# Laying a fallback program ahead of the main code, and moving set-up off VectorE, in a fused attention and gated-MLP kernel

## The chip, the cores and the metric

The kernel runs on one core of one Trainium2 chip. The metric is the device time of one execution in microseconds (us). A figure with "median" is the median of several executions on the chip; every figure taken from a trace belongs to one profiled execution and counts from the start of its span. In the lines of the profile PE is TensorE, PEld its weight loads, ACT ScalarE, DVE VectorE, POOL GpSimd and SP SyncE, which in this kernel only issues transfers; PSUM is the memory of the tiles that the profile calls `ps`, which the matmuls write here (`PE MATMUL ps<-...`). TensorE's clock is a share of full speed, 1.0 or 0.5 in these traces, as the trace records it. A fetch is a packet that the trace lists on a queue of the kind "instruction", 8 or 16 KB each within the span; the 16 KB ones that stand beside jumps are put down to TensorE.

## The reference, cut to what matters

```python
x  = A_x                                  # (1, 2048, 512) bf16
xn = layernorm(x)
return x + attention(xn, wqkv, wo) + gated_mlp(xn, w1, w3, w2)
# attention: 32 heads of 16, softmax over 2048 keys
# gated_mlp: (silu(xn @ w1) * (xn @ w3)) @ w2, inner size 1792
```

The softmax needs 32 x 2048 x 2048 exponentials. The kernel computes most of them on ScalarE (790 instructions of 128x1024) and the rest (234) on VectorE with an integer approximation. That approximation is only right for scores in a range, so the kernel holds a second, slower and exact program, the fallback, and a flag that tells at the end which result stands. With these inputs the fallback is never run.

## The kernel before: the parts that matter

A planner in Python simulates the five engines with a table of durations and decides, before the kernel is built, in which order each engine's instructions stand. Its state is a clock and, for each engine, the time when it is free. It is greedy: what is ready first is placed first.

```python
class _Sched(_Prog):
    def __init__(self):
        ...
        self.free = {e: 0.0 for e in _ENGS}
    ...
    def _time(self, op, deps, dur, tail, mode=None, rows=None):
        ready = self._ready(op, deps)
        if op.eng != "pe":
            start = max(self.free[op.eng], ready)
            ...
```

The set-up, at the very start, is put on VectorE: a matrix of ones for TensorE's warm-up, the clear of a PSUM bank, three small mask operations, and a probe of what VectorE makes of 70000 in an integer conversion.

```python
P.op("dve", lambda e: e.memset(ones_t[:, :], 1.0), writes=[("ones_t",)], dur=0.1)
P.op("dve", lambda e: e.memset(bank(7), 0.0), writes=[("ps", 7)], dur=0.6)
# ... three mask operations, then the probe:
P.op("dve", lambda e: e.memset(satv[:, :], 70000.0), writes=[("satv",)], dur=0.1)
P.op("dve", lambda e: e.tensor_scalar(satn[:, :], satv[:, :], YB, G_LO, ALU.add, ALU.max), ...)
P.op("dve", lambda e: e.tensor_scalar(accb[:, 3:4], satn[:, :], 32767.0, None, ALU.is_equal), ...)
# ...
keep_warm(WARM, 0.107)      # warm-up matmuls for TensorE's clock
```

SyncE issues all loads and stores from one queue, in the planned order, and waits in that queue (in the profile before for up to 2.33 us at a time). Two kinds of issue matter below: the weights of the MLP in pairs, and the broadcast of the softmax's reciprocals, which has to wait until a small transfer, Rrow, has landed.

```python
def load_w13(idx):          # a pair of weight loads
    P.dma(lambda e: e.dma_start(w13[:, sl, 0:DC, :], w1_v[...]), writes=[("w13", sl, 0)], kb=128)
    P.dma(lambda e: e.dma_start(w13[:, sl, DC:2 * DC, :], w3_v[...]), writes=[("w13", sl, 1)], kb=128)

def e4():                   # a group of four broadcasts
    for j in range(4):
        q = P.dma(lambda e, j=j: e.dma_start(R[...], Rrow[j:j + 1, :]...broadcast_to([1, 16, 512])),
                  reads=[("Rrow",)], writes=[("R", j, h)], kb=32)
```

At the end every engine loads the flag and jumps over its part of the fallback, which lies between its main code and its end:

```python
def run(name, e):
    PF.emit_engine(name, e, sems[0][0], sems[0][1])          # main code
    e.wait_ge(sems[0][0]["dve"], flag_op.token[1])
    reg = e.alloc_register("slow_" + name)
    e.reg_load(reg, flag[0:1, 0:1])
    with e.If(e.snap(reg) > 0):
        ...                                                  # fallback
    PF.emit_end(name, e, sems[0][1])                         # SyncE waits for the outputs here
```

## Time and profile before

| | value |
|---|---|
| median of three runs, before the prediction | 787.33 us (785.9 to 787.77) |
| medians of the kernel before in the later jobs | 787.11, 787.61, 787.33, 787.62, 787.25 us |
| profiled execution | 785.95 us, span 784.14 us |
| TensorE's first real work, a transpose | 6.82 us |
| first exponential on ScalarE | 11.77 us |
| last VectorE operation to the end of the span | 5.18 us |

The lines of this profile that carry the argument stand in the prediction.

### The profile page before, as it was taken

The page shows a single profiled execution, that of the slowest core. Times are in us where ns is not written, and L with a number is a line of the kernel's source. Part 1 is how long each engine was busy: PE and PEld are TensorE (multiplying, and loading weights), DVE is VectorE, ACT ScalarE, POOL GpSimd, SP SyncE. Part 2 cuts the span into 40 slices and gives each one's busy share as a digit, 9 for nine tenths or more (in the row PEclk, how much of TensorE's full clock was granted, in tenths as well). Part 3 has the DMA queues.
Part 4 walks back from the last instruction along what each step waited for, and adds up shares of the span by engine and source line. Part 5 has one row for each costly group of instructions (what it writes and reads, how often), then busy time and mean ns, then how long its engine had stood idle before and what let it go on. Part 6 is the DMA issues. An engine that isn't in the chain of part 4 may idle for free.

```text
span 784.1 us, 21514 instructions
## 1 busy us (share of the span) xinstructions
PE 735.2 (94%) x9361; PEld 233.0 (30%) x9361; DVE 761.3 (97%) x872; ACT 764.2 (97%) x865; POOL 93.7 (12%) x120
## 2 busy tenths in 40 slices
PE   8999999999999999998899999998898999999996
PEld 6422222222222222222222322222222232222234
DVE  8899999999999999999999999999999999999995
ACT  6999999999999999999999999999999999999994
POOL 3200031102011020301102020110200202110000
PEclk9999999999999999999999999999999999999998
DMA  7023123213342213333403223332332212332202
GB/s 216 3 22 117 7 29 36 33 28 48 47 55 16 40 20 49 48 36 50 61 17 42 36 30 49 48 41 45 36 49 29 42 24 36 50 44 20 15 19 45
DMA packets 83440, 32.93 MB, mean 42 GB/s; under 512 B 72072, under 2 KB 79496, under 8 KB 83336
## 3 DMA queue, kind: packets, MB, share of 16 engines
q1 hardware_dynamic: 83336, 31.46, 28.0%
q8 instruction: 75, 1.23, 0.7%
q14 instruction: 29, 0.24, 0.1%
HBM read 22.81 MB, written 2.10 MB: 32 GB/s over the span
## 4 chain that ended last, share of the span: by engine, by line
ACT 82%; PE 10%; DVE 6%; issue 1%; DMA 0%; POOL 0%; DVEq 0%; ACTq 0%
ACT f_PT L1879 78%; PE ps L1338 3%; ACT f_th L1564 3%; PE ps L1809 3%; PE ps L2083 2%; DVE f_xd L1956 2%; DVE f_xd L2005 1%; DVE f_xd L1998 1%; DVE f_xd L2014 1%; DVE f_t L1568 0%; DVE f_hT L1578 0%; DMA f_xd<-in_A_x_dram 0%; DVE f_xd L2020 0%; PE ps L1350 0%; DVE f_stats L1262 0%
## 5 line engine op out<-in xcount | busy, mean ns | idle before, releaser
L1879 ACT ACTIVATE f_PT<-ps 128x1024 bf16<-128x1024 f32 x790 | 737.9, 1107 | 2.1 <-PE ps L1809 2.0
L1809 PE MATMUL ps<-f_QT,f_KT 32*128 32x512 bf16 (+1 forms) x2112 | 292.8, 378 | 29.6 <-ACT f_PT L1879 23.2
L1956 DVE TENSOR_SCALAR f_xd<-ps 128x1024 int16<-128x1024 f32 x234 | 284.6, 1216 | 7.1 <-PE ps L1809 7.0
L2083 PE MATMUL ps<-f_PT,f_Vaug 128*17 128x512 bf16 (+2 forms) x1628 | 208.8, 377 | 6.0 <-DVE f_xd L2005 2.2
L2083 PE MATMUL ps<-f_xd,f_Vaug 128*17 128x512 bf16 (+2 forms) x1452 | 196.2, 376 | 2.1 <-DVE f_U L2103 1.2
L1809 PEld LDWEIGHTS ps<-f_QT,f_KT 32*128 32x128 bf16 x2112 | 75.4, 91 | 305.5 <-ACT f_PT L1879 237.5
L1338 PE MATMUL ps<-f_xnT,f_w 128*32 128x512 bf16 x1792 | 137.1, 383 | 2.9 <-DVE f_t L1568 1.5
L2005 DVE TENSOR_TENSOR f_xd<-f_xd 128x3072 bf16<-128x3072 bf16 (+1 forms) x79 | 137.3, 1738 | 0.0
L1480 POOL TENSOR_SCALAR f_QT<-f_QT,f_msk 128x256 bf16<-128x256 bf16 x60 | 57.9, 965 | 292.6 <-DVE f_xd L2020 88.7
L1998 DVE TENSOR_SCALAR f_xd<-f_xd 128x3072 int16<-128x3072 int16 (+1 forms) x79 | 74.8, 947 | 1.1
L2083 PEld LDWEIGHTS ps<-f_PT,f_Vaug 128*17 128x17 bf16 (+1 forms) x1628 | 54.2, 92 | 69.9 <-issue 37.8
L2014 DVE TENSOR_SCALAR f_xd<-f_xd 128x3072 int16<-128x3072 int16 (+1 forms) x79 | 74.4, 942 | 0.0
L2020 DVE TENSOR_SCALAR f_xd<-f_xd 128x3072 int16<-128x3072 int16 (+1 forms) x79 | 74.2, 939 | 0.0
L1338 PE MATMUL ps<-f_w,f_hT 128*32 128x512 bf16 x896 | 71.5, 383 | 0.0
L2144 POOL TENSOR_TENSOR f_onorm<-f_U,f_R 128x256 bf16<-128x256 f32 x30 | 25.3, 850 | 344.7 <-DMA f_R<-f_Rrow 262.7
L2083 PEld LDWEIGHTS ps<-f_xd,f_Vaug 128*32 128x32 bf16 (+1 forms) x1452 | 50.5, 92 | 52.3 <-issue 32.8
L1338 PEld LDWEIGHTS ps<-f_xnT,f_w 128*32 128x32 bf16 x1792 | 39.2, 94 | 59.3 <-issue 44.2
L1578 DVE SCALAR_TENSOR_TENSOR f_hT<-f_t,ps 128x512 bf16<-128x512 bf16 x56 | 37.9, 676 | 0.2
L1568 DVE SCALAR_TENSOR_TENSOR f_t<-f_th,ps 128x512 bf16<-128x512 f32 x56 | 37.8, 675 | 0.1
L1564 ACT ACTIVATE f_th<-ps 128x512 f32<-128x512 f32 x56 | 37.6, 672 | 0.0
L1338 PEld LDWEIGHTS ps<-f_w,f_hT 128*32 128x32 bf16 x896 | 19.2, 95 | 23.0 <-issue 16.6
L1338 PE MATMUL ps<-f_wo,f_onorm 128*32 128x512 bf16 x272 | 21.9, 382 | 0.0
(84 smaller groups left out, 239.2 us busy)
## 6 DMA issues: line engine op xcount, KB each, us to landing
f_w<-in_B_w_dram SPq DMA_DIRECT2D x112, 128.0 KB, 4.3
f_R<-f_Rrow SPq DMA_DIRECT2D x124, 32.0 KB, 4.5
f_xr<-in_A_x_dram SPq DMA_DIRECT2D x16, 128.0 KB
f_U<-f_U SPq DMA_DIRECT2D x60, 32.0 KB, 2.0
f_w<-in_B_w_dram SPq DMA_DIRECT2D x7, 256.0 KB
f_xd<-in_A_x_dram SPq DMA_DIRECT2D x3, 512.0 KB
out_dram<-f_xn_sb SPq DMA_DIRECT2D x12, 128.0 KB, 3.6
f_xd<-in_A_x_dram SPq DMA_DIRECT2D x2, 256.0 KB
```

The costliest lines, as they stand in the source:

```text
L1338: ins = e.matmul(bank(bk)[32 * i:32 * i + 32, 0:ncols], make_lhsT(i), rhs_ap, start=start, stop=stop, tile_position=(0, 32 * i))
L1480: q = P.op("pool", lambda e: e.tensor_scalar(QT[:, d_, cs], QT[:, s1, cs], msk[:, h:h + 1], None, ALU.mult), reads=[("QT", s1), ("msk", h) ...
L1564: q = P.op("act", lambda e: e.activation(th[:, ss, :], bank(bk), ACTF.Tanh, scale=0.5), reads=[("ps", bk)], writes=[("th", ss)], dur=a_cos ...
L1578: q = P.op("dve", lambda e: e.scalar_tensor_tensor(hT[:, idx % NH, :], t1[:, ss, :], 0.5, bank(bk), ALU.mult, ALU.mult), reads=[("t1", ss) ...
L1809: ins = e.matmul(b, l_, r_, start=True, stop=True, tile_position=(rp, 0))
L1879: q = P.op("act", lambda e: e.activation(PT[:, s_, :], ps[:, b0 * 512:(b0 + 2) * 512], ACTF.Exp, scale=ASC, bias=ABIAS), reads=[("ps", b0) ...
L1956: q = P.op("dve", lambda e: e.tensor_scalar(dsl[:, ys, 1024 * c:1024 * c + 1024], ps[:, b0 * 512:b0 * 512 + 1024], YB, G_LO, ALU.add, ALU. ...
L1998: P.op("dve", lambda e: e.tensor_scalar(dsl[:, NY + m_, 0:n], y, 0x7F, 0x3F00, ALU.bitwise_and, ALU.bitwise_or), reads=YK, writes=[("ds", ...
L2005: q_ = P.op("dve", lambda e: e.tensor_tensor(t_ap.bitcast(BF16), y.bitcast(BF16), t_ap.bitcast(BF16), ALU.mult), reads=YK + [("ds", NY + m ...
L2014: q_ = P.op("dve", lambda e: e.tensor_scalar(g_ap, y, -G_LO, 0.0, ALU.add, ALU.max), reads=YK, writes=[("g", g_, k) for k in range(n // 51 ...
L2020: q_ = P.op("dve", lambda e: e.tensor_scalar(y, y, 0x7F80, None, ALU.bitwise_and), reads=YK, writes=YK, dur=s_cost(n), name="e", lock=True)
L2083: ins = e.matmul(bank(PV)[32 * j:32 * j + (17 if g % 2 == 0 else 32), pc], v_, p_, start=s0, stop=s1, tile_position=(0, 32 * j))
```

## The change

Its intent: each engine's jump over the fallback takes 2.6 to 4.6 us at the end. Lay the fallback in front, so that the end follows the main code directly, and jump over it near time zero, where the engines are thought to be idle. To make room for VectorE's jump, take the set-up off VectorE. The diff, cut:

```diff
+JUMP = {"pe": 2.5, "act": 2.5, "dve": 2.9, "pool": 4.4}
@@ set-up
-        P.op("dve", lambda e: e.memset(bank(7), 0.0), writes=[("ps", 7)], dur=0.6)
-        ... three mask operations and three probe operations on "dve"
+        P.op("act", lambda e: e.activation(bank(7)..., ones_t..., ACTF.Copy, scale=0.0), ...)
+        ... four mask operations on "pool"
+        P.cut = {k: len(P.ops[k]) for k in _ENGS}
+        for k in ("pe", "act", "dve", "pool"):
+            P.free[k] = max(P.free[k], JUMP[k])
+        def sat_probe():
+            ...                       # the three probe operations, still on "dve"
+        P.post("dve", sat_probe, ready=60.0, prio=1)
@@ def run(name, e):
-            PF.emit_engine(name, e, sems[0][0], sems[0][1])
-            ...
-            with e.If(e.snap(reg) > 0):
+            n = PF.cut[name]
+            PF.emit_engine(name, e, sems[0][0], sems[0][1], 0, n)      # set-up
+            e.br("main_" + name)                                       # the far jump
+            with nc.body("slow_" + name, valid_engines=[e.engine]):
                 ...                                                    # fallback
+                e.br("end_" + name)
+            with nc.body("main_" + name, valid_engines=[e.engine]):
+                PF.emit_engine(name, e, sems[0][0], sems[0][1], n, None, known)
+                PF.emit_end(name, e, sems[0][1])
+                ...                                                    # flag, near branch
```

More of the change, by code (lines that the diff above doesn't have):

```diff
@@ L107, in check, with emit_engine @@
             assert len(kinds) <= 1, "engine %s mixes DMA and compute ops" % e
-    def emit_engine(self, e, handle, sems, dma_sems):
-        known = {}
-        for op in self.ops[e]:
+    def emit_engine(self, e, handle, sems, dma_sems, first=0, last=None, known=None):
+        known = dict(known or {})
+        for op in self.ops[e][first:last]:
             need = {}
@@ L1203, in _plan_fast @@
         P.op("dve", lambda e: e.memset(ones_t[:, :], 1.0), writes=[("ones_t",)], dur=0.1)
-        P.op("dve", lambda e: e.memset(bank(7), 0.0), writes=[("ps", 7)], dur=0.6)
-        P.op("dve", lambda e: e.tensor_reduce(msk[:, 1:2], msk4[:, :], AX.X, ALU.add), reads=[("msk4",)],
-             writes=[("msk", 1)], dur=0.1)
-        P.op("dve", lambda e: e.tensor_scalar(msk[:, 0:1], msk[:, 1:2], -1.0, 1.0, ALU.mult, ALU.add),
-             reads=[("msk", 1)], writes=[("msk", 0)], dur=0.1)
-        P.op("dve", lambda e: e.tensor_scalar(mskq[:, :], msk[:, :], QS, None, ALU.mult),
-             reads=[("msk", 0), ("msk", 1)], writes=[("mskq",)], dur=0.1)
-        P.op("dve", lambda e: e.memset(satv[:, :], 70000.0), writes=[("satv",)], dur=0.1)
-        P.op("dve", lambda e: e.tensor_scalar(satn[:, :], satv[:, :], YB, G_LO, ALU.add, ALU.max),
-             reads=[("satv",)], writes=[("satn",)], dur=0.1)
-        P.op("dve", lambda e: e.tensor_scalar(accb[:, 3:4], satn[:, :], 32767.0, None, ALU.is_equal),
-             reads=[("satn",)], writes=[("acc", 3)], dur=0.1)
+        P.op("act", lambda e: e.activation(bank(7).rearrange("p (a n) -> p a n", a=4),
+                                           ones_t[:, :].unsqueeze(1).broadcast_to([128, 4, 128]), ACTF.Copy, scale=0.0),
+             reads=[("ones_t",)], writes=[("ps", 7)], dur=0.6)
         P.op("pool", lambda e: e.affine_select(ident[:, :], ones_t[:, :], [[1, 128]], ALU.is_equal, 0.0,
@@ L1219, in _plan_fast @@
         P.op("pool", lambda e: e.memset(mhalf[:, :], -0.5), writes=[("mhalf",)], dur=0.1)
+        P.op("pool", lambda e: e.tensor_tensor(msk4[:, 0:2], msk4[:, 0:2], msk4[:, 2:4], ALU.add), reads=[("msk4",)],
+             writes=[("msk4",)], dur=0.1)
+        P.op("pool", lambda e: e.tensor_tensor(msk[:, 1:2], msk4[:, 0:1], msk4[:, 1:2], ALU.add), reads=[("msk4",)],
+             writes=[("msk", 1)], dur=0.1)
+        P.op("pool", lambda e: e.tensor_scalar(msk[:, 0:1], msk[:, 1:2], -1.0, 1.0, ALU.mult, ALU.add),
+             reads=[("msk", 1)], writes=[("msk", 0)], dur=0.1)
+        P.op("pool", lambda e: e.tensor_scalar(mskq[:, :], msk[:, :], QS, None, ALU.mult),
+             reads=[("msk", 0), ("msk", 1)], writes=[("mskq",)], dur=0.1)
         P.op("pool", lambda e: e.memset(Vaug[:, :, :, 16:17], 1.0),
              writes=[("V", t, i) for t in range(NT) for i in range(2)], dur=1.2)
+        P.cut = {k: len(P.ops[k]) for k in _ENGS}
+        for k in ("pe", "act", "dve", "pool"):
+            P.free[k] = max(P.free[k], JUMP[k])
+        def sat_probe():
+            P.op("dve", lambda e: e.memset(satv[:, :], 70000.0), writes=[("satv",)], dur=0.1)
+            P.op("dve", lambda e: e.tensor_scalar(satn[:, :], satv[:, :], YB, G_LO, ALU.add, ALU.max),
+                 reads=[("satv",)], writes=[("satn",)], dur=0.1)
+            P.op("dve", lambda e: e.tensor_scalar(accb[:, 3:4], satn[:, :], 32767.0, None, ALU.is_equal),
+                 reads=[("satn",)], writes=[("acc", 3)], dur=0.1)
+        P.post("dve", sat_probe, ready=60.0, prio=1)
         def keep_warm(n, dur):
@@ L2346, in run @@
         def run(name, e):
-            PF.emit_engine(name, e, sems[0][0], sems[0][1])
-            e.wait_ge(sems[0][0]["dve"], flag_op.token[1])
-            reg = e.alloc_register("slow_" + name)
-            e.reg_load(reg, flag[0:1, 0:1])
-            with e.If(e.snap(reg) > 0):
+            n = PF.cut[name]
+            PF.emit_engine(name, e, sems[0][0], sems[0][1], 0, n)
+            known = PF.known
+            e.br("main_" + name)
+            with nc.body("slow_" + name, valid_engines=[e.engine]):
                 for k in _ENGS:
@@ L2359, in run @@
                 PM.emit_end(name, e, sems[1][1])
-            PF.emit_end(name, e, sems[0][1])
+                e.br("end_" + name)
+            with nc.body("main_" + name, valid_engines=[e.engine]):
+                PF.emit_engine(name, e, sems[0][0], sems[0][1], n, None, known)
+                PF.emit_end(name, e, sems[0][1])
+                e.wait_ge(sems[0][0]["dve"], flag_op.token[1])
+                reg = e.alloc_register("slow_" + name)
+                e.reg_load(reg, flag[0:1, 0:1])
+                e.br_cmp(reg, 0, on_true="end_" + name, on_false="slow_" + name, comp_op="IS_LE")
+            nc.switch_bb("end_" + name)
         with nc.Block() as block:
```

## The prediction

> **What bounds the kernel now.** I read the page first, then the timeline of the first 14 us and of the last 12, then the branch and flag lines one by one, because the change touches only those two ends.

> ```profile
> PE 735.2 (94%) x9361; PEld 233.0 (30%) x9361; DVE 761.3 (97%) x872; ACT 764.2 (97%) x865; POOL 93.7 (12%) x120
> ...
> ACT 82%; PE 10%; DVE 6%; issue 1%; DMA 0%; POOL 0%; DVEq 0%; ACTq 0%
> ```

> ScalarE and VectorE are both busy 97% of 784.1 us; the chain that ended last is mostly ScalarE's exponentials. ScalarE is idle about 20 us in all. The table of stretches places them: 6.9 before 12 us, 1.1 between 12 and 30, about 11 after 772, next to nothing between. So a delay of the first exponential is paid in full unless something in 12 to 30 us gives it back, and a cut after the last output is a pure gain. The start, from the timeline:

> ```profile
> 0.88 0.17 DVE L1203 MEMSET f_ones_t<- 128x128 bf16 x1 [0.88 <-PEq L2409]
> ...
> 1.11 5.82 PE L1225 MATMUL ps<-f_ones_t 128*128 128x128 bf16 x68 [1.11 <-DVE f_ones_t L1203]
> ...
> 3.57 1.29 DVE L1262 BATCH_NORM_STATS2 f_stats<-f_xd 128x6 f32<-128x512 bf16 x2 [0.30 <-DMA f_xd<-in_A_x_dram]
> ...
> 5.17 0.19 POOL L1235 TENSOR_SCALAR f_lnt<-f_mv 128x2 f32<-128x2 f32 x1 [2.33 <-DVE f_mv L1268]
> ...
> 6.82 0.72 PE L1350 MATMUL ps<-f_ident,f_xn_sb 128*128 128x128 bf16 x8
> ...
> 11.77 1.02 ACT L1879 ACTIVATE f_PT<-ps 128x1024 bf16<-128x1024 f32 x1 [0.49 <-PE ps L1809]
> ```

> VectorE waits for x until 3.57, ScalarE for the transposes until 7.25. TensorE looks idle but is not: its 68 warm-up matmuls fill 1.11 to 6.76, and the first transpose follows at once at 6.82. The end, from the views of the flag and branch lines:

> ```profile
> L2350 SPq TENSOR_LOAD <-flag x1: 557/557/557, 779.4 to 779.4; - x1
> ...
> L2351 PEldq COMPARE_BRANCH  x1: 4575/4575/4575, 778.5 to 778.5; - x1
> ...
> L2351 SPq COMPARE_BRANCH  x1: 55/55/55, 780.1 to 780.1; - x1
> ...
> L2362 POOLq DRAIN  x1: 122/122/122, 781.1 to 781.1; - x1
> L2362 ACTq DRAIN  x1: 66/66/66, 782.0 to 782.0; - x1
> L2362 DVEq DRAIN  x1: 57/57/57, 782.5 to 782.5; - x1
> ...
> L142 SPq EVENT_SEMAPHORE  x3: 28/28/28, 782.9 to 783.7; - x3
> ```

> Each engine loads the flag and jumps over the fallback; its next instruction comes 2.6 us later on GpSimd, 3.4 on ScalarE, 3.5 on VectorE, 4.6 on TensorE and 2.8 on SyncE (780.14 to 782.94). But SyncE then still waits for the last output transfer, whose record is complete at 783.67. The jump is thus nearly hidden by the transfer. The transfer itself is late: of its 16 completions twelve are in by 781.08, the others come at 781.76, 781.99, 782.47 and 783.67. In exactly that stretch, 779.39 to 783.81, the trace holds eight 8 KB instruction packets on one queue and a 16 KB one that took 1.86 us (0.88 to 1.44 for that queue's earlier ones).

> [...] the records of the branches themselves are 45 to 72 ns, [...] except on TensorE whose record includes it. [...] Here the spacing drops from 107 to 56 ns 3.8 us after the first, at 4.92.

> **The change part by part.**

> End, removed: the five far jumps. Now the end block follows the main code, so the branch stays near. Also, SyncE now waits for the output transfers before it loads the flag, where before it did so while they ran. Without fetches I take the landing at 781.1 to 781.5 (twelve of sixteen were there at 781.08). Then: flag load 0.56 with 0.03 before it, 0.13 to the compare as before, compare 0.06, one more near branch 0.05, and the old rest from the completed wait to the end, 784.14 - 783.68 = 0.46. Sum 1.29, end at 782.4 to 782.8 instead of 784.14: a gain of 1.35 to 1.75, call it 1.6. That is less than half of TensorE's 4.6 us, because the output transfer is behind it.

> Start, moved there: the same jumps. The planner's new table says engines are free at 2.5 (TensorE, ScalarE), 2.9 (VectorE), 4.4 (GpSimd); its zero is the first load's issue, 0.79 in the trace, so 3.3, 3.7 and 5.2.
> - VectorE: one memset stays, then the jump to about 3.7, against 3.57 for x. Cost 0 to 0.9. Its removed set-up (0.48 for the clear, 2 us of small operations up to 3.28) ended before x came: worth nothing but room for the jump. The three probe operations go to about 60 us, some 0.4 us among other work.
> - GpSimd: four small operations of 0.15 to 0.2 more, then 1.2 us of memset beside the jump; 5.2 against 5.17 needed. Cost about 0.
> - ScalarE: the clear (estimated 0.5, as a 512-column activation takes about 0.5) lies behind the table load that ends at 2.06; needed at 7.25. Cost 0. GpSimd's masks are ready by about 3, needed at 10.2.
> - SyncE jumps after its first loads at 6.3; the weights behind it come 3 us later, first needed far after 30. Cost 0.
> - TensorE: the order of instructions has nothing before its jump, and again 68 warm-up matmuls before the first transpose. In the planner's code the start of a TensorE operation is its inputs' readiness and the last matmul's start, not the engine's free time, so the 2.5 does not thin them out. They begin at 3.3 instead of 1.1 and take about 5.65 again (36 cold, 32 warm): first transpose at 8.95 instead of 6.82, 2.1 later. The second pair, the K and Q products and the first exponential follow in the same static order, at about 13.8. ScalarE's idle 1.1 us and VectorE's 2 us or so between 12 and 30 may return 0.3 to 0.6. Net cost 1.6, between 0.8 and 3.

> Middle: the planner re-rolls its order. Counts in the program: 790 and 234 exponentials as before; one 128x384 eviction moves from VectorE to ScalarE (0.4 us); waits differ by a few. I take 0 with 1 us either way.

> Sum: 787.33 - 1.6 + 1.6 = 787.3; I shade it to 787.2, since the jump constants look measured and the author may have got a shorter start than I infer.

> **The rivals.**
> (1) The start is really idle: the jump costs nothing, 785.7. For it: the DVE, GpSimd and ScalarE rows above, with 2 to 6 us of waiting. Against it: TensorE's row, gapless to the first transpose.
> (2) Instruction fetch delays the x loads. The first load's 16 completions end at 3.55; at the end of the kernel fetches made a transfer up to 2.6 us late. If x comes 1 us late, the transposes are ready near 7.8, still behind TensorE's 8.95, so it hides; if 2.5 us late, it is the bound and the time is about 788.
> (3) TensorE's jump takes 4.6 us as at the end: first transpose after 11, 4 us late, 789.5. Against it: at the end five jumps and an output ran together; at the start it goes first, before any data packet (the first is at 2.19).
> (4) The gain at the end is larger: if landing were not late, 1.75 is the limit.
> (5) The re-rolled order dominates: one us either way, hidden or shown by the run-to-run spread of 1.9 us.

> **Range and chances.** Start 0.8 to 3, end -1.35 to -1.75, middle and noise 1 each: in quadrature about 1.7, so 785.0 to 789.5. Two per cent is 15.7 us; both ends together hold about 20 us of idle time and the change can reach at most some 5. Faster 0.01, same 0.98, slower 0.01.

> **What would show it.** Right: warm-up matmuls starting near 3.3, first transpose near 9 with no wait on VectorE, first exponential near 13.5; at the end, no gap of over 1 us after any branch, outputs landing about 2.1 us after issue with all 16 completions close together, and about 1.3 us from landing to end. Wrong: first transpose still near 7 (then the start was idle), warm-up matmuls fewer cold, x landing after 5, or the last instruction still 4 us after the last output's issue. If ScalarE's idle time between 12 and 750 us changes by over 1 us, the re-roll mattered and my zero for the middle was wrong.

Cut from this text, and marked in it, are statements about the hardware that no trace of this case shows. No term of the sum is among them: it stands at 787.33 - 1.6 + 1.6 = 787.3, shaded to 787.2. Read from the trace of the kernel before: the records of the branches at its end, where TensorE's of 4.58 us holds the whole jump, and the spacing of the warm-up matmuls, from which come the 36 cold and 32 warm ones of the sum. The 0.05 us for one more near branch is an estimate from those records (45 to 72 ns). That fetches held up the last output was its reading of their times (the completions ran on from 781.08 to 783.67 while fetches were under way), not shown by itself.

## More of the kernel before

In SyncE's timeline of the kernel before (start, duration, queue, line, operation, tiles, count) the eighth group of broadcasts looks like this:

```profile
218.78 0.62 SPq L2128 DMA_DIRECT2D f_Rrow<-f_Rc  x1
219.44 0.47 SPq L1315 DMA_DIRECT2D f_w<-in_B_w_dram  x1
220.01 0.45 SPq L1317 DMA_DIRECT2D f_w<-in_B_w_dram  x1
220.86 2.42 SPq L2133 DMA_DIRECT2D f_R<-f_Rrow  x4
```

SyncE issues Rrow, then uses the time in which Rrow travels for one pair of weight loads, and only then issues the four broadcasts, which had to wait for Rrow anyway.

## The result, and the profile after

The changed kernel takes 792.65 us (median of 6 runs, 791.55 to 793.76) against 787.11 for the kernel before in the same rounds. The ratio is 1.0072, with a 95% interval of 1.0057 to 1.0088. A ratio here is the mean time of one kernel's runs over that of the other's in the same rounds, so it is not quite the ratio of the two medians. The prediction, 787.2 with a range to 789.5, was wrong: the change costs 5.5 us. The class "within 2%" held, but only because it is nearly three times as wide as the loss.

The page of the changed kernel, busy times and the chain that ended last:

```profile
PE 734.3 (93%) x9361; PEld 230.8 (29%) x9361; DVE 759.8 (96%) x867; ACT 767.0 (97%) x867; POOL 95.6 (12%) x124
...
ACT 73%; PE 11%; DVE 10%; DMA 2%; issue 2%; SPq 1%; POOL 0%; DVEq 0%; POOLq 0%; ACTq 0%
```

The engines did nearly the same work (ScalarE's busy time is 2.8 us longer, see the end of the account below). But ScalarE's share of the chain fell from 82 to 73 per cent, and "DMA 2%" and "SPq 1%" are new: somewhere the kernel now waits for transfers and for SyncE's queue. The start, from the timeline of the changed kernel and from the line of TensorE's jump:

```profile
0.89 0.17 DVE L1204 MEMSET f_ones_t<- 128x128 bf16 x1 [0.89 <-PEq L2429]
...
5.23 6.56 PE L1237 MATMUL ps<-f_ones_t 128*128 128x128 bf16 x68 [5.23 <-issue]
...
5.37 1.29 DVE L1274 BATCH_NORM_STATS2 f_stats<-f_xd 128x6 f32<-128x512 bf16 x2 [4.32 <-DMA f_xd<-in_A_x_dram]
...
6.96 0.19 POOL L1247 TENSOR_SCALAR f_lnt<-f_mv 128x2 f32<-128x2 f32 x1 [3.10 <-DVE f_mv L1280]
...
11.63 0.61 PE L1362 MATMUL ps<-f_ident,f_xn_sb 128*128 128x128 bf16 x8
...
16.36 1.02 ACT L1891 ACTIVATE f_PT<-ps 128x1024 bf16<-128x1024 f32 x1 [0.49 <-PE ps L1821]
```

```profile
L2387 PEldq COMPARE_BRANCH  x1: 4303/4303/4303, 0.9 to 0.9; - x1
```

TensorE's jump alone took 4.30 us, so its warm-up matmuls began at 5.23 instead of 1.11. VectorE waited for x until 5.37 instead of 3.57. The first exponential came 4.6 us later than before. The end, from the views of the flag, branch and end lines:

```profile
L2378 SPq TENSOR_LOAD <-flag x1: 491/491/491, 791.2 to 791.2; - x1
...
L2379 DVEq COMPARE_BRANCH  x1: 61/61/61, 788.4 to 788.4; - x1
L2379 ACTq COMPARE_BRANCH  x1: 39/39/39, 788.7 to 788.7; - x1
L2379 SPq COMPARE_BRANCH  x1: 49/49/49, 791.7 to 791.7; - x1
...
L2382 DVEq DRAIN  x1: 41/41/41, 788.5 to 788.5; - x1
...
L142 SPq EVENT_SEMAPHORE  x3: 17/28/28, 789.0 to 791.0; - x3
```

Here everything is as intended: after its branch each engine goes on at once (VectorE from 788.43 to its drain at 788.5, where before it took 3.5 us), and the last output, issued at 788.56, has landed at 791.01. From the last VectorE operation to the end it is 3.50 us instead of 5.18.

So far the start has lost 4.6 and the end won 1.7, which does not make 5.5. The rest lies in the middle. This is the table of stretches for 225 to 250 us and 330 to 345 us, first of the kernel before, then of the changed one. The columns are the stretch, its length, the busy time of TensorE, its weight loads, VectorE, ScalarE and GpSimd (with counts), TensorE's granted clock, the DMA engines' share and GB/s:

```profile
225.00:250.00 25.00, 23.30 (x280) 6.95 (x272) 23.71 (x26) 25.00 (x29) 5.15 (x6) 1.00 0.31 36
330.00:345.00 15.00, 13.33 (x164) 4.20 (x160) 14.80 (x17) 15.00 (x19) 0.92 (x1) 1.00 0.45 55
```

```profile
225.00:250.00 25.00, 21.72 (x248) 5.92 (x250) 21.70 (x24) 22.41 (x26) 5.14 (x6) 0.93 0.31 38
330.00:345.00 15.00, 13.24 (x148) 3.54 (x148) 14.31 (x16) 14.17 (x17) 3.69 (x4) 0.89 0.13 28
```

ScalarE, the bound, was busy without a gap in both stretches before. Now it stands still for 2.59 us in the first and 0.83 in the second, and TensorE's clock is below full in both. The view of waits for 215 to 245 us names the cause, TensorE waiting for a weight load (total, times, longest):

```profile
PE ps L1350 <- DMA f_w<-in_B_w_dram: 2.1, 1, 2.1
```

And SyncE's timeline there shows why that load is late:

```profile
222.22 0.62 SPq L2140 DMA_DIRECT2D f_Rrow<-f_Rc  x1
224.28 2.42 SPq L2145 DMA_DIRECT2D f_R<-f_Rrow  x4
226.74 0.59 SPq L1327 DMA_DIRECT2D f_w<-in_B_w_dram  x1
```

Compare this with the four lines of the kernel before. The pair of weight loads that used to be issued while Rrow travelled now stands behind the broadcasts. SyncE waits 1.4 us for Rrow with nothing else to do, takes 2.4 us for the broadcasts, and the pair, whose first load is issued at 226.74, lands at 231.3, after TensorE wanted it. Then TensorE's clock drops to one half for 3.41 us, from 232.57 to 235.99, and once more from 338.38 to 341.80. No such window lies between 5 and 779 us of the profile before.

The two profiled executions lie near opposite ends of their kernels' times (785.95 is low, 793.76 the highest), so their difference, 7.8 us, is larger than that of the medians. The experiments therefore separate the parts with five rounds each.

### The profile page after: what moved, and what is told of

Same layout as the page of the kernel before. It is cut to its first block, busy times and chain, and to the rows that moved or that the text cites. A ratio compares the mean times of both kernels' runs of the same rounds, so it can differ in the third digit from the quotient of the medians.

```text
span 792.0 us, 21515 instructions
## 1 busy us (share of the span) xinstructions
PE 734.3 (93%) x9361; PEld 230.8 (29%) x9361; DVE 759.8 (96%) x867; ACT 767.0 (97%) x867; POOL 95.6 (12%) x124
## 4 chain that ended last, share of the span: by engine, by line
ACT 73%; PE 11%; DVE 10%; DMA 2%; issue 2%; SPq 1%; POOL 0%; DVEq 0%; POOLq 0%; ACTq 0%
ACT f_PT L1891 69%; DVE f_xd L1968 4%; PE ps L1350 4%; PE ps L1821 3%; ACT f_th L1576 3%; PE ps L2095 3%; DVE f_xd L2017 2%; DVE f_xd L2026 1%; DVE f_xd L2010 1%; PE ps L1237 1%; DVE f_xd L2032 1%; SPq L2145 1%; DMA f_Rrow<-f_Rc 1%; DMA f_w<-in_B_w_dram 1%; DMA f_R<-f_Rrow 1%
## 5 line engine op out<-in xcount | busy, mean ns | idle before, releaser
L2095 PE MATMUL ps<-f_PT,f_Vaug 128*17 128x512 bf16 (+2 forms) x1628 | 205.9, 378 | 3.2 <-ACT f_PT L1891 1.1
L2095 PE MATMUL ps<-f_xd,f_Vaug 128*17 128x512 bf16 (+2 forms) x1452 | 192.3, 378 | 3.5 <-DVE f_xd L2017 1.0
L1350 PE MATMUL ps<-f_xnT,f_w 128*32 128x512 bf16 x1792 | 136.8, 385 | 4.5 <-DMA f_w<-in_B_w_dram 2.1
L2095 PEld LDWEIGHTS ps<-f_PT,f_Vaug 128*32 128x32 bf16 (+1 forms) x1628 | 52.4, 92 | 62.4 <-issue 39.5
L1350 PE MATMUL ps<-f_w,f_hT 128*32 128x512 bf16 x896 | 69.0, 382 | 0.0
L2156 POOL TENSOR_TENSOR f_onorm<-f_U,f_R 128x256 bf16<-128x256 f32 x30 | 26.6, 896 | 336.8 <-DMA f_R<-f_Rrow 143.3
L2095 PEld LDWEIGHTS ps<-f_xd,f_Vaug 128*32 128x32 bf16 (+1 forms) x1452 | 48.1, 92 | 54.3 <-issue 29.9
L1350 PEld LDWEIGHTS ps<-f_xnT,f_w 128*32 128x32 bf16 x1792 | 38.7, 95 | 60.5 <-issue 43.3
L1350 PEld LDWEIGHTS ps<-f_w,f_hT 128*32 128x32 bf16 x896 | 19.2, 95 | 23.7 <-issue 16.2
L1350 PE MATMUL ps<-f_wo,f_onorm 128*32 128x512 bf16 x272 | 22.8, 383 | 0.8 <-DVE f_fm L2301 0.7
```

Source lines behind the costliest of these rows:

```text
L1350: ins = e.matmul(bank(bk)[32 * i:32 * i + 32, 0:ncols], make_lhsT(i), rhs_ap, start=start, stop=stop, tile_position=(0, 32 * i))
L2095: ins = e.matmul(bank(PV)[32 * j:32 * j + (17 if g % 2 == 0 else 32), pc], v_, p_, start=s0, stop=s1, tile_position=(0, 32 * j))
```

## The experiments

All kernels gave right results. Each ran with five rounds beside the kernel before of its own job, each job on another chip, so that kernels of different jobs are best compared by their ratios. layout_only, order_only, pe_fallback_behind and hinted ran in one job (before: 787.61), order_swap, after_swap, probe_only and few_warm in the next (787.33), late_w, no_fallback, warm40 and probe_at_start in the third (787.62), pinned and mended in the last (787.25).

### layout_only and order_only: the change cut in two

The change does two things: it lays the program out differently, and it gives the planner a different set-up to plan with. layout_only takes the new layout with the planner and set-up of before; order_only takes the new planner and set-up with the layout of before.

```diff
 layout_only: before, with run() and emit_engine() of the changed kernel
+        P.cut = {k: len(P.ops[k]) for k in _ENGS}
+        P.cut["dve"] = 1
 order_only: the changed kernel, with run() of before
```

> The kernel before with only the fallback moved in front and jumped over: its own order of instructions, its own set-up (VectorE jumps after its first memset). My theory: the changed kernel loses 4.6 us at the start because TensorE leaves its jump at 5.2 and then still runs 68 warm-up matmuls, wins 1.7 at the end, and loses 2.5 to 3 in the middle to the re-rolled order. Then this one starts its first exponential near 16.4, ends 3.5 us after the last VectorE operation, and takes before + 2.9: 790.0 (789.2 to 790.8). Rival, the order is to blame for all and the moved jumps cost nothing net: 787.1 within 0.7.

> The changed kernel's planner (with its table of jump times) and its set-up off VectorE, but the fallback behind the main code as before. My theory: first exponential near 11.8 as before, the end 5.2 us after the last VectorE operation, and what is over is the price of the re-rolled order, 2.5 to 3 us: 789.7 (788.8 to 790.5). Rival, the order is worth nothing and the 2 us stall for weights seen in one profile is chance: 787.1 within 0.7.

layout_only: 787.12 us, ratio 1.0008 (0.9986 to 1.0029). order_only: 791.69 us, ratio 1.005 (1.0031 to 1.007). Both expectations missed. layout_only was expected at 790.0 and came out at the rival's 787.1; order_only was expected at 788.8 to 790.5 and came out above that. The net effect of the layout is not told from zero; the order of the instructions, which no line of the diff mentions, costs about 4 us (that it is the order, and not the set-up that order_only moves as well, is shown by probe_only below). In order_only's trace the stall of the changed kernel is there again, with ScalarE busy for 21.27 of the 25 us:

```profile
225.00:250.00 25.00, 21.25 (x256) 6.00 (x252) 20.99 (x24) 21.27 (x25) 4.24 (x5) 0.93 0.26 42
```

In layout_only's trace the same stretch has ScalarE at 25.00 and a full clock; its first exponential comes at 15.09, its last VectorE operation ends 3.17 us before the end, and its last exponential ends 3.04 us later than before. It is the predicted exchange of start against end; the sizes are taken up further below.

### pe_fallback_behind: is it TensorE's jump?

Kernel layout_only, with TensorE's fallback left behind its main code, so that TensorE alone jumps at the end.

```diff
+            if name == "pe":
+                PF.emit_engine(name, e, sems[0][0], sems[0][1])
+                ...                           # flag, branch, fallback, as before
+                return
```

> As layout_only, but TensorE alone keeps its fallback behind its main code and jumps at the end. My theory: TensorE's jump plus the warm-up behind it is the binding delay at the start, and its 16 KB fetch is what made the last sixteenth of the first x load late (5.35 instead of 3.55). So warm-up starts at 1.1 again, x lands by 4.3, the first exponential comes at 12 to 12.8; the end is like before's or up to 1 us better, as TensorE's fetch again meets the output. Time 787.0 (786.2 to 788.2). Rival, the other engines' jumps and late loads delay the start just as much: first exponential past 15 and 789.5 or more.

788.97 us, ratio 1.0021 (1.0002 to 1.0041). This is above the range expected; the rival's late first exponential (past 15) did not come either, it is at 13.78. TensorE has done its warm-up matmuls at 7.45 us (6.8 before), but its first transpose comes at 8.83, since VectorE's statistics start only at 5.59. The timeline of VectorE:

```profile
0.88 0.17 DVE L1203 MEMSET f_ones_t<- 128x128 bf16 x1 [0.88 <-PEq L2437]
4.34 0.48 DVE L1204 MEMSET ps<- 128x512 f32 x1 [3.29 <-issue]
...
5.59 1.28 DVE L1265 BATCH_NORM_STATS2 f_stats<-f_xd 128x6 f32<-128x512 bf16 x2
```

The statistics have no wait in brackets; what precedes them is VectorE's own jump, until 4.34, and then 1.25 us of set-up. The completions of the first x load end at 4.28 in this trace. The late landing, 5.2 to 5.4 us in layout_only and in the changed kernel, comes with TensorE's 16 KB fetch in the traces, which this one does not have at the start. So with the jump in front, taking the set-up off VectorE is right in itself; in the changed kernel x then lands at 5.35 and hides what it gains. The gain at the end is gone in this kernel, because TensorE's jump of 4.2 us is back there.

### hinted: keep the layout, hide the jump

The kernel before, with a branch hint some instructions ahead of each engine's jump.

```diff
+            if i == len(self.ops[e]) - HINT[e]:
+                self.loc = handle.mark_branch_hint_location()
...
+            e.br_cmp(reg, 0, on_true="end_" + name, on_false="slow_" + name,
+                     comp_op="IS_LE").branch_hint(loc, "LikelyTaken")
```

> The kernel before, order and layout unchanged, but each engine gets a branch prefetch hint some 5 to 20 us before its far jump at the end. If the end's cost is the fetch of the jump's target and its collision with the last output transfer, then the fetch happens early, the jump takes under 0.5 us, the 16 completions of the last output come together, and the end moves from 5.2 us after the last VectorE operation to 2.9 to 3.5: time 785.1 (784.5 to 785.8), start unchanged. Rival, the hint is not followed or is dropped: 787.1 within 0.7, jumps of 2.6 to 4.6 us as before.

787.38 us, ratio 0.9996 (0.9975 to 1.0018): nothing, as the rival said. All five engines executed their hint, at 766 to 773 us (GpSimd's at 711.6, 68 us ahead of its jump and not 5 to 20 as meant). It worked on TensorE alone, whose branch took

```profile
L2356 PEldq COMPARE_BRANCH  x1: 415/415/415, 780.0 to 780.0; - x1
```

instead of 4.58 us. The four others still needed 2.6 us (GpSimd) to 4.0 us (VectorE) to their next instruction, and the last output landed at 784.89.

### order_swap and after_swap: one pair of loads put back

If the late pair makes the loss, two instructions moved in SyncE's queue must bring it back.

```diff
+        S = P.ops["sp"]
+        at = [i for i, o in enumerate(S) if o.name == "R"][4 * 7]     # eighth group of broadcasts
+        S[at:at + 6] = S[at + 4:at + 6] + S[at:at + 4]                # the pair goes ahead of it
```

> Kernel order_only with one pair of weight loads issued by SyncE ahead of the eighth group of four R broadcasts instead of behind it, nothing else. Theory (the new order costs its time at one place: the late pair makes TensorE wait 2.8 us, and the pause brings two windows of 3.4 us at half clock): the pair lands before TensorE asks for it, the wait at about 228 us and the windows at half clock at 228 and 334 us are gone, and some 3 us of order_only's extra 4 come back: 788.5 us against 791.7 for order_only. Rival (the cost is spread over the order, the wait is only where it shows): the wait goes or moves, the time stays at 791 to 792.

> The changed kernel with the same one pair of weight loads ahead of the same group of R broadcasts. Theory: as in order_swap some 3 us come back: 789.5 us, the wait and the two slow clock windows gone, what is left being the late start less the gain at the end. Rival: 792 to 793 us as without the swap.

order_swap: 788.56 us, ratio 1.0013 (0.9995 to 1.003), 3.1 us less than order_only by the medians, 2.9 by the ratios. after_swap: 789.59 us, ratio 1.0025 (1.0008 to 1.0043), 3.1 us less than the changed kernel by the medians, 3.7 by the ratios. ScalarE is busy through the whole stretch in order_swap:

```profile
225.00:250.00 25.00, 23.57 (x298) 6.93 (x294) 24.66 (x28) 25.00 (x29) 4.23 (x5) 1.00 0.34 36
```

One part of the expectation missed: only the slow window at 228 us is gone. The one at about 333 stayed in both kernels (331.9 and 333.4), and order_swap's profile has another at 65.7.

### late_w: the same pair, moved the other way

The mirror image: the kernel before, with its pair at 219.44 us moved behind the broadcasts. Nothing else differs from the kernel before.

```diff
+        S[at:at + 6] = S[at + 2:at + 6] + S[at:at + 2]
```

> The kernel before with one pair of weight loads moved behind the eighth group of R broadcasts in SyncE's queue, the reverse of order_swap, nothing else. Theory (this one place in SyncE's order makes most of the loss): TensorE waits 2 to 3 us for the pair at about 225 us, a window of 3.4 us at half clock follows, and the time is 790 to 791 us against 787.3. Rival (the wait hurts only in the new order, because the work around it is laid differently): TensorE or ScalarE catch up, 787 to 788 us.

792.62 us, ratio 1.0061 (1.0043 to 1.0079). TensorE waits 3.1 us for the pair, and ScalarE loses 4.5 us of the stretch (the line of waits for 215 to 245 us, and the stretch):

```profile
PE ps L1339 <- DMA f_w<-in_B_w_dram: 3.1, 1, 3.1
...
225.00:250.00 25.00, 20.50 (x212) 5.43 (x204) 19.27 (x22) 20.50 (x24) 4.93 (x6) 0.86 0.27 42
```

This is more than expected (790 to 791). In the profiled execution the stall was followed by slow windows at 228.7 and 245.7, and two more lay at 143.3 and 583.6. Two loads in the wrong place cost this kernel as much as the whole change.

### probe_only and probe_at_start: what turned the order over

Comparing the planned orders showed that the JUMP table moves nothing: the kernel before with only the table added plans exactly as before, and the changed kernel without the table plans exactly as with it. What moves the order are three tiny operations. Plans rebuilt from these kernels confirm it: probe_only and the changed kernel have one and the same order on TensorE and SyncE, and on the other engines they differ by the moved set-up alone. probe_only is the kernel before with nothing changed but the time at which the planner may place the saturation probe. probe_at_start is the changed kernel with the probe at the start.

```diff
 probe_only, against before
-        P.op("dve", ...memset(satv...)); P.op("dve", ...satn...); P.op("dve", ...accb[:, 3:4]...)
+        P.post("dve", sat_probe, ready=60.0, prio=1)
 probe_at_start, against the changed kernel
-        P.post("dve", sat_probe, ready=60.0, prio=1)
+        sat_probe()
```

> The kernel before, with only the three tiny VectorE operations of the saturation probe handed to the planner with a ready time of 60 us in place of the start; no table, no change of layout, no operation on another engine. SyncE's order is then that of the changed kernel. Theory (the planner's new order is the cost): 791.5 us, with the wait for a weight load at about 228 us, although nothing but 0.4 us of VectorE's work has moved. Rival (the set-up on GpSimd, or running it late, is the cost): 787 to 788 us.

> The changed kernel with the three operations of the saturation probe put right behind VectorE's jump instead of at 60 us: same layout, same set-up off VectorE, but the planner draws a third order. Theory (start and end are those of the changed kernel, together 1 to 2 us above before or even, and the rest is the luck of the order): no wait for the weight pair at about 230 us unless this order has its own such place, 787 to 790 us. Rival (set-up off VectorE or the table makes any such plan worse): 792 to 793 us.

probe_only: 792.57 us, ratio 1.0072 (1.0053 to 1.0091), as much as the changed kernel, with no jump moved and no work added. Its trace has ScalarE at 21.40 of 25 us between 225 and 250, and a slow window at 227.1. Three operations of 0.4 us together, put at 60 us, change what the planner finds free next, and 160 us later a pair of loads stands behind a group of broadcasts. probe_at_start: 789.97 us, ratio 1.0033 (1.0014 to 1.0051), with no such wait between 225 and 250 (ScalarE 24.79) but with a stall and a slow window of its own at 80 us, where ScalarE stands still for 2.0 us at 80.9 and for 0.8 us at 83.4. It is a third draw of the order, with its own weak place.

### few_warm and warm40: a shorter start

In layout_only the jump ends at 5.1 us and 68 warm-up matmuls then take 5.3 us, while the normalised x is ready at 8.44. few_warm runs 16 of them ahead of the first transpose (and 2 in place of the 8 that stand between the two sets of transposes), warm40 runs 40.

```diff
 few_warm
-                for i in range(n):
+                for i in range(8 if n == WARM else 1):
 warm40
+                for i in range(8 if n == WARM else n):
```

> Kernel layout_only with 28 warm-up matmuls in place of 68 (20, then eight times 1). Theory (TensorE reaches the first transpose late because its jump ends at 5.1 us and the warm-ups then take 5.3 us): the first transpose waits for x alone and starts at 8.5 to 8.9 us instead of 10.4, the first exponential at 13.3 to 13.7 instead of 15.1, and the time is 785.5 us, 1.5 below layout_only and below the kernel before. Rival (the warm-ups pay for themselves: with fewer of them the clock is still low when the real work begins): the first exponential comes no earlier than 14.5 and the time stays at 787.

> Kernel layout_only with 40 warm-up matmuls in place of 68 ahead of the first transpose (few_warm had 16), the later ones untouched. Theory (16 were too few to raise the clock, 68 last longer than x takes): the 40 end at about 8.3 us, the clock is full by then, the first transpose starts at 8.5 to 8.8 us, the first exponential at 13.4 to 13.7, and the time is 785.5 us, below both kernels. Rival[...]: first exponential at 14.5 to 15.3, 786.5 to 787.5 us.

The text for few_warm says 28 (20, then eight times 1); the kernel that ran has 16 (8, then eight times 1) ahead of the first transpose. few_warm: 789.72 us, ratio 1.003 (1.0011 to 1.0049), above the kernel before; against layout_only, whose interval overlaps, it is not shown. Its timeline of TensorE:

```profile
4.87 1.89 PE L1228 MATMUL ps<-f_ones_t 128*128 128x128 bf16 x16 [4.87 <-DVE ps L1204]
8.85 1.03 PE L1353 MATMUL ps<-f_ident,f_xn_sb 128*128 128x128 bf16 x8 [2.09 <-DVE f_xn_sb L1252]
```

The first transpose comes at 8.85 as expected, but eight of them take 1.03 us instead of 0.61: the clock is low and stays so until 13.7 us. The first exponential is at 15.34, later than with 68. warm40: 788.34 us, ratio 1.0015 (0.9995 to 1.0035); first transpose at 9.08, still on the low clock, which rose at 10.76, and first exponential at 14.29. In both the clock was still low when the real work began, as few_warm's rival had it; the reason that warm40's rival gave is cut from its text, since it was not shown. The times came out longer than the rivals said (789.72 against 787, 788.34 against 786.5 to 787.5), and the start does not explain this: few_warm's first exponential is only 0.25 us later than layout_only's and warm40's is 0.8 earlier. few_warm's profiled execution, its slowest, also has slow clock windows at 146.8 (a double one) and 167.3. Fewer warm-up matmuls won nothing here; that 40 are worse than 68 is not shown, since the intervals overlap.

### no_fallback: the end alone

The kernel before, without the fallback and without its branch: right for these inputs, but not a kernel to use.

```diff
-            with e.If(e.snap(reg) > 0):
-                ...
```

> The kernel before without the fallback program and without its branch; right for these inputs, but not a kernel to use. It has the cheap end without any jump at the start. Theory (the far jumps cost 1.7 us at the end, and in front they cost the same at the start): output lands 2.1 us after its issue, end 1.1 us later, 785.5 us; layout_only less this, 1.6 us, is the price of the jumps at the start. Rival (the end gains nothing, because the output's landing sets it anyway): 787 us.

785.4 us, ratio 0.9975 (0.9952 to 0.9997). The last output lands 2.1 us after its issue (780.92 to 783.04). This measures what the end has to give: 2.0 us (0.2 to 3.8). By the trace, from the last VectorE operation to the end it is 2.63 us here, against 3.17 in layout_only, where SyncE loads the flag only after the outputs have landed. With nearly the same end and a ratio of 1.0008, layout_only pays about as much for the jumps in front as its end gives.

### pinned and mended: the change with the order held

The order can be held by giving the planner, behind the moved set-up, the engines' free times of the kernel before. pinned has the whole change but the late probe: the set-up on GpSimd and ScalarE, the probe behind VectorE's jump, all jumps in front, and exactly before's order of everything else. mended is pinned with TensorE's fallback behind its main code and the hint on its branch.

```diff
+        P.cut = {k: len(P.ops[k]) for k in _ENGS}
+        P.cut["dve"] = 1
+        P.free.update({"act": 0.0, "dve": 1.819, "pool": 2.368})
```

> The change with the order of before held: set-up of masks and PSUM clear moved to GpSimd and ScalarE, far jumps in front, but the planner is given the engines' free times of the kernel before, and the probe stays behind VectorE's jump at the start; the order of all other instructions is then exactly before's. Theory (the change's own parts even out, and the order made the whole loss): x lands at 5.3 us and VectorE waits for it, first transpose at 10.4, first exponential at 15.1, end 3.2 us behind the last VectorE operation, 787 us, within 0.2% of before and 5 us below the changed kernel. Rival (the moved set-up costs on GpSimd or ScalarE): 789 us or more.

> As pinned, but TensorE keeps its fallback behind its main code, with the prefetch hint on its branch that worked at the end of the kernel hinted. Theory (at the start, TensorE's own jump of 4.2 us costs most; without its fetch x lands at 4.3 us, as in pe_fallback_behind, where 1.3 us of set-up behind VectorE's jump hid it): statistics start at 4.7 us, first transpose at 7.9, first exponential at 13.0, TensorE's last branch under 0.5 us, so 1.7 us won at the end against 1.2 lost at the start: 786.6 us, 0.1% below before, at the limit of what five rounds tell. Rivals: the hint fails with the other engines' jumps gone, 4 us at the end, 788.5 us; or GpSimd's jump, begun at 2.5 us, ends behind 6.5 and holds up the coefficients: first transpose at 8.8, 787.3 us.

pinned: 789.09 us, ratio 1.0027 (1.0008 to 1.0046). This fits the rival's "789 or more" better than the theory's 787, but the trace shows no cost of the set-up on GpSimd or ScalarE: VectorE waits for x until 5.39 (as written), TensorE's warm-ups begin at 5.23, and nothing waits for a mask. What differs from layout_only is that the clock rose at 9.67 us instead of 8.18, the 68 warm-up matmuls took 5.9 us instead of 5.3, and the first exponential came at 15.85 instead of 15.09. That is 0.8 us; the rest of the 2 us between the medians lies within the two intervals and stays open. In any case pinned is 3.6 us below the changed kernel by the medians, 3.5 by the ratios, with the order as the only larger difference.

mended: 788.13 us, ratio 1.0013 (0.9991 to 1.0035). The theory had 786.6. Its start is as the theory has it and the best of all kernels with jumps in front: x lands at 4.27, statistics at 4.49, first transpose at 7.72, first exponential at 12.68. TensorE's last branch takes 0.41 us. But from the last VectorE operation to the end it is 5.04 us: a 16 KB fetch of TensorE now runs from 781.88 to 783.33, 0.75 us behind the end of its branch, while the last output is under way. Fifteen of the output's sixteen parts have landed by 783.45, the sixteenth at 785.34. The hint took the wait from TensorE, but a fetch still ran beside the output. Without a hint the kernel before has two such fetches there, one from 779.41, during the branch, and one from 783.69, 0.65 us behind its end. By its time the one that is left is the second; what it carries the trace does not say. That this fetch made the sixteenth part late is likely (pe_fallback_behind has the same, 2.0 us, with a 16 KB fetch beside it), but was not tested by itself. Neither rival had it.

No kernel tried here that keeps the fallback beats the kernel before.

## Why the prediction was wrong

**The end: right.** It predicted no gap after any branch, landing about 2.1 us after issue, and 1.3 us from landing to the end; the changed kernel has 2.4 and 1.0 (layout_only 2.1 and 1.0). In the changed kernel two misses of 0.3 us cancel. Predicted gain 1.6; measured 1.7 by the tail of its trace (5.18 to 3.50), and 2.0 in layout_only's (to 3.17).

**The start: right in mechanism, wrong in size.** It saw that TensorE is not idle at the start and that its jump is paid for. The mis-sized term is "they begin at 3.3 instead of 1.1": the author's table was taken for a measurement, and the jump measured 4.30 us. Rival (3) had the right size and was set aside because "at the start it goes first, before any data packet (the first is at 2.19)". That was a misreading: in the trace of before, which it read, the first packet of x starts at 1.80 and ends at 2.19. In the changed kernel the packets of x start at 1.79, and the 16 KB fetch runs from 1.85 to 3.78 beside them. Then "take about 5.65 again" came out at 5.2 to 6.4, depending on when the clock rose. The first transpose was predicted at 8.95 and came at 11.63, the first exponential at 16.36 instead of 13.8. Of this delay nearly nothing is regained: layout_only is 3.3 us late at the first exponential and still 3.0 at the last. Where the text estimated a net start cost of 1.6, it is 3.0 in layout_only's trace and 4.1 to 4.6, before the little that is regained, in pinned's and the changed kernel's. In layout_only's trace, 3.0 lost at the start and 2.0 won at the end make +1.0, and its ratio allows for that.

Rival (2), x late beside the fetches, came true as well (5.35 instead of 3.55), but was hidden behind TensorE, as the text argued.

**The middle: the step that failed.** "The planner re-rolls its order ... I take 0 with 1 us either way." The order cost about 4 us: 3.9 by order_only's ratio (2.4 to 5.5), 4.1 by the medians. Of it 3.1 us hang on one pair of loads in SyncE's queue, shown from both sides: put back, it brings back 3.1 us by the medians, 2.9 and 3.7 by the ratios (order_swap, after_swap); moved in the order of before, it costs 5.0 by the medians (late_w). Rival (5) named the order, but at one us either way. The number of operations on each engine, which the prediction counted, says nothing about this. Part of what would have told was in reach without a chip. The trace of before shows that the broadcasts hold the queue for over 2 us and that the next pair, issued at 223.33, lands more than 4 us later. But comparing SyncE's planned order of the two kernels gives candidates, not the answer: of 31 groups of broadcasts, five (the 5th, 8th, 14th, 15th and 19th) lose the pair that stood between Rrow and the broadcasts, and six gain one. In the trace of the changed kernel TensorE waits for a pair of the eighth group only.

The prediction named the right test: if ScalarE's idle time between 12 and 750 us changed by over 1 us, its zero was wrong. It went from 1.6 to 5.6 us, some of it at the late start; from 30 to 750 us it went from 0.5 to 3.7, and the two stretches shown account for that (3.4).

**The sum.** By ratios, with 787 us: layout_only +0.6 (-1.1 to +2.3), order_only +3.9 (2.4 to 5.5), together +4.5; the changed kernel +5.7 (4.5 to 6.9). The intervals leave room for 1 us or so of a start that is longer in the changed kernel than in layout_only, as its trace has it.

**The slow clock windows.** They add to the loss, but not alike in every execution (the mean clock of the kernel before runs from 0.991 to 1.000). In the changed kernel the two slow ones last 3.413 us each and begin 65.0 and 96.0 times that after the first rise of the clock at 10.71. The count here goes in such steps from the first rise in each trace: the sixteen traces hold 3567 such windows between the first full clock and 770 us. For each I took the share in which TensorE has a matmul in the records. Twenty windows were themselves at half clock and are left out; one of these, busy for 93%, was followed by another (few_warm). Below 0.63, nine of ten windows were followed by one at half clock; from 0.63 to 0.66, six of eleven; from 0.66 to 0.70, two of 23; from 0.70 to 0.85, two of 500; above, none of 3003. Each of the four stalls of over 2 us at full clock (changed kernel, order_only, late_w, probe_only) was followed by a slow window. One window with no gap over 0.53 us was followed by one too, at a share of 0.56 (probe_at_start). The share alone does not decide it, as one window at 0.633 was followed by full clock (pinned) and others at 0.633 by half (hinted, late_w). That this explains the spread of one kernel's executions is plausible, as the longer ones have the lower mean clock (the kernel before at 785.46 us had 0.998, at 790.81 it had 0.991), but it was not tested by itself.

What stays open: why pinned is 2 us above layout_only in the medians, of which its trace explains 0.8; and what the rest of the new order costs, order_swap still being at 1.0013 with the pair put back. Two things are in the traces: the slow window at about 333 us, which stayed in both swapped kernels (ScalarE was idle there for 1.1 us in order_swap), and ScalarE's busy time, 766.1 to 767.0 us in all five traces of the new order against 763.8 to 765.2 in the ten of the old. One eviction more (0.5 us) and, outside probe_only, the clear (0.6) are part of that; what each costs was not tested.

## What to carry to other kernels

Where a greedy planner lays out the program, every change is also a new draw of the order, and its luck can be larger than the effect that one wants to measure: three operations of 0.4 us cost 5 us. Hold the order fixed when judging a change, compare the orders of the DMA queue before and after, look for loads that have slipped behind an issue which must wait, and ask of each how soon it is needed: four of the five here made TensorE wait for nothing. A jump isn't free because an engine looks idle. In front it cost TensorE 3.8 to 4.3 us and VectorE 3.1 to 3.6, and beside TensorE's fetch the first load of x was complete at 4.9 to 5.4 us instead of 3.6 to 4.1. Warm-up matmuls are work: 68 of them took 5.2 to 6.4 us.
